# Idle products on a constant, one small product in wider tiles, and a rounding step split by block

## The chip, the cores and the metric

The kernel runs on one core of a Trainium2 chip. The metric is the device time of one execution in microseconds, lower is better. "Span" is the stretch from the first to the last instruction in a profiled execution.

## The reference

Attention with a polynomial sketch (4 batches, 4 heads, 1088 rows, head size 32), then a feed-forward block with an ELU:

```
phi(x) = outer(S1 x, S2 x)                     # 8 x 8 = 64 features
kv = sum_s phi(k_s) v_s^T ;  z = sum_s phi(k_s)
x  = (phi(q) kv) / (phi(q) . z + 1e-6)         # heads side by side: 4352 x 128
h  = x @ w_in                                  # 128 x 2048
out = ELU(h) @ w_out                           # 4352 x 128
```

S1, S2, w_in and w_out arrive as 64-bit floats; the kernel rounds them to 32-bit floats itself, by integer operations on the two words of each number.

## The kernel before

**Tiles and stages.** Rows are worked in groups `g` of 512 (the last of 256). The feed-forward block's 2048 hidden columns are 8 blocks `cp` of 256. For each (g, cp) `mm1` makes `h` in two PSUM banks, `elu` makes `gg` from it (two activations on ScalarE, one VectorE operation), and `mm2`, `mm2_blocks` or `mm2_seven` adds the output product. `steps` lists the pairs (g, cp); the products of a step are written out two steps after its `mm1`.

**Order.** The schedule is manual: each engine runs its instructions in the order in which the program writes them. Ahead of the loop over `steps` stands a prologue written out by hand: features of k and q of the first batch, their sums, the first two groups' queries and the rounding of the first weight blocks. Inside the loop the tables `extra` (filled by `at`, `mid`, `late`) say at which step the other batches' work is put in.

**Tiles of the array.** A product in `quarters` is cut into column tiles of `width[0]` columns (32 at first, 64 from step 30 on); so are `mm2_blocks` and `mm2_seven`. The feature products of the prologue (`KF`, `q1_first`, `q1z_first`, `q1_second`) use tiles of 64 columns, the queries inside the loop tiles of 32 or 64 rows and columns. A 32-bit product is two instructions (two passes) on TensorE for each column tile.

**Idle products.** `keep_warm(n, cols)` issues products of ones in the full 128 x 128 array, whose result in `idle` nobody reads. They stand at the very start (ahead of `sps`, the first product that counts), after `Z(0)`, after the sums of k and v, and ahead of `mm1_first`. Their operand `some` is a 128 x 256 tile that VectorE fills first of all.

**Prologue around the change.** `sps` and `SXps` need `Sx` (rounded S1 and S2). `Sab` comes from `sps`; `KF(0)` makes the features of k in `abp` from `Sab` and the transposed `kT`; `Z_first` sums them into `zps` and copies the sums to `zl`. `Z(0)` multiplies `zl` by `SXh` with `quarters`; `Z_out` writes the masked result into `SW`, from which `q1z_first` makes `zqp`, the denominators' part for the first group's queries. `q2_den` multiplies (`pw`), sums and inverts it (`den`), `q2_out` makes the query features `qp`; `q4_early` transposes them (`qtp`, `qpT`), `q5_early` makes `xps` and `xg`, the input of `mm1`.

**Rounding.** `order` numbers pieces of the weights: 0 and 1 are the w_in halves of blocks 0 and 1, 2 the w_out half of block 0, 3 that of block 1, and so on. `RA`, `RB` make the power of two (VectorE, ScalarE), `RS`, `RM`, `RD` the mantissa, and `RE` multiplies both into `W`. `RC_2` does the last four for pieces 0 and 1 together, in VectorE operations of 512 columns; `RC(i)` does them for one piece.

Of the kernel before, what the change touches and what calls it, by code (L numbers as in the profile page):

```python
# [12 lines left out]
F32 = mybir.dt.float32  # L13
# [9 lines left out]
def _ap(ap: bass.AP, free):  # L23
    return dataclasses.replace(ap, ap=[list(ap.ap[0])] + [list(x) for x in free])
# [3 lines left out]
def kernel(  # L28
# [21 lines left out]
    nc = tc.nc  # L50
    B, H, S, D = q.shape
    R = S1.shape[0]
    P = 128
# [10 lines left out]
    const = ctx.enter_context(tc.tile_pool(name="const", bufs=1))  # L64
# [20 lines left out]
            src = v[b].rearrange("h (y t) d -> y h t d", t=NT)[:, :, t0:t1, :]  # L85
            eng.dma_start(vt[b][r, :VN].rearrange("p (h t d) -> p h t d", h=H, t=KT)[:, :, :t1 - t0, :], src)

    some = const.tile([P, 256], F32, name="some")
    nc.vector.memset(some[:], 1.0)
    idr = const.tile([P, 2 * R, R], F32, name="idr")  # L90
    nc.vector.memset(idr[:], 0.0)
    Sx = const.tile([P, H, D], F32, name="Sx")
# [87 lines left out]
    def round_w(f, i, *a):  # L180
        if wide:
            cp, w_in, w_out = order[i]
            c = slice(0 if w_in else 2 * P, 4 * P if w_out else 2 * P)
            f(raw_w[cp][:, c], W[:, cp, c], *a)

    def RA(i):
        round_w(round_a, i)
# [4 lines left out]

    def RC_2():
        if wide:
            for f in (round_s, round_m, round_d, round_e):
                f(raw_2[:, :, :2 * P], W[:, :2, :2 * P])

    def RS(i):
# [8 lines left out]
    def RE(i):  # L207
        round_w(round_e, i)
# [41 lines left out]
    idle = psum.tile([P, 512], F32, name="idle", tag="o0", bufs=1)  # L250
# [2 lines left out]

    width = [32]

    def quarters(dst, lhs, rhs, **kw):
        for c in range(0, P, width[0]):
            nc.tensor.matmul(dst[c:c + width[0]], lhs[:, c:c + width[0]], rhs, skip_group_check=True,  # L258
                             tile_position=(0, c), **kw)

    def keep_warm(n, cols=256):
        for i in range(n):
            nc.tensor.matmul(idle[:, :cols], some[:, :P], some[:, :cols], skip_group_check=True)  # L263


    nc.gpsimd.tensor_copy(idr[:R], _ap(ident[:R, :R], [[0, 2 * R], [1, R]]))
# [14 lines left out]
    SXh = const.tile([P, FD], F32, name="SXh")  # L281
# [12 lines left out]
    SWq = const.tile([FD, B, 2, 4, R], F32, name="SWq")  # L294
    SWs = const.tile([FD, B - 1, 4, R], F32, name="SWs")
    keep_warm(3)
    keep_warm(1, 128)
    sps = psum.tile([P, 512], F32, name="sps", tag="aux")
    nc.tensor.matmul(sps[:, :2 * R], Sx[:].rearrange("p h d -> p (h d)"), ident[:, :2 * R])
    make_SXh()  # L300
# [102 lines left out]
    def KO_first(t0, t1):  # L403
        half, o = divmod(t0, 5)
        n = t1 - t0
        a_ = kf_ps[half][:, 64 * o:64 * (o + n)].rearrange("p (m x r) -> p m x r", x=2, r=R)[:, :, 1, :]
        b_ = feats[0][:, 0, t0:t1].rearrange("p t h r -> p (t h) r")
        nc.vector.tensor_mul(feats[0, half][:, o:o + n].rearrange("p t h i j -> p (t h) i j"),
                             _ap(a_, list(a_.ap[1:]) + [[0, R]]), _ap(b_, [[R, n * H], [0, R], [1, R]]))
# [30 lines left out]

    def Z(b, ps, zl):

        quarters(ps[:, 96:128], SXh[:], zl[:])

    def Z_out(b, ps):
        z = wzs[b] = SW[:, :, 2, :] if b == 0 else work.tile([FD, H, R], F32, name="wz", tag="wz")[:]
# [22 lines left out]
    def Z_first():  # L469
        ps = psum.tile([P, 512], F32, name="zps", tag="h", bufs=4)  # L470
        for i in range(KT):
            z_tile(0, ps, i)
        return ps, ZC(0, ps)
# [46 lines left out]
    def q1z_first():  # L520
        p = psum.tile([P, 512], F32, name="zqp", tag="h", bufs=4)
        for i in range(4):
            for u in range(2):
                b, t = half_tile(0, 2 * i + u)
                nc.tensor.matmul(p[64 * u:64 * u + 64, i * 32:i * 32 + 32].rearrange("p (h r) -> p h r", h=H),
                                 qT[b][:, t, :], SW[:, :, 2, :], skip_group_check=True, tile_position=(0, 64 * u))
        return p[:, :128].rearrange("p (t h r) -> p h t r", t=4, h=H)
# [58 lines left out]
            nc.vector.transpose(abw[g][:, m * r:m * r + m, :].rearrange("p m y -> p (m y)"),  # L586
                                ps[r][:, o:o + 32 * m])

    def q2(g, parts=1):
        q2_den(g)  # L590
        q2_out(g, parts)

    def q2_den(g, zq=None):
        m = H * (un[g] if g > 1 else qn[g])
        x = abw[g][:, :m, :]
        pw = pws[g % 2]
        if zq is None:
            nc.vector.tensor_mul(pw[:, :m, :R], x[:, :, R:2 * R], x[:, :, 2 * R:3 * R])
        else:
            nc.vector.tensor_mul(pw[:, :m, :R].rearrange("p (h t) r -> p h t r", h=H),  # L600
                                 x[:, :, R:2 * R].rearrange("p (h t) r -> p h t r", h=H), zq)
        den = work.tile([P, 8 * H], F32, name="den", tag="den")
        nc.vector.tensor_reduce(den[:, :m], pw[:, :m], axis=AX, op=ADD)
        nc.vector.reciprocal(den[:, :m], den[:, :m])
        an = work.tile([P, 8 * H, R], F32, name="an", tag="an")
        nc.vector.tensor_mul(an[:, :m], x[:, :, R:2 * R], _ap(den[:, :m], [[1, m], [0, R]]))
        ans[g] = an

    def q2_out(g, parts=1, between=None):
        m = H * qn[g]  # L610
        x, an = abw.pop(g), ans.pop(g)
        qp[g] = work.tile([P, 4 * H, R, R], F32, name="qp", tag="qp", bufs=2)
        for i in range(parts):
            if i and between:
                between()
            h = slice(i * m // parts, (i + 1) * m // parts)
            a_ = an[:, h]
            b_ = x[:, h, :R]
            nc.vector.tensor_mul(qp[g][:, h], _ap(a_, list(a_.ap[1:]) + [[0, R]]),
                                 _ap(b_, [b_.ap[1], [0, R], b_.ap[2]]))  # L620
# [13 lines left out]
    def q5_early(g):  # L634
        xp = [psum.tile([P, 512], F32, name="xps", tag="aux") for _ in range(2)]
        for h in range(H):
            for w in range(2):
                nc.tensor.matmul(xp[w][D * h:D * h + D, :256], kvS[64 * w:64 * w + 64, h, :],  # L638
                                 qpT[g][64 * w:64 * w + 64, h].rearrange("p m s -> p (m s)"),
                                 skip_group_check=True, tile_position=(64 * w, D * h))  # L640
        xg[g] = work.tile([P, 512], F32, name="xg", tag="xg", bufs=3)
        to = xg[g][:].rearrange("p (m w s) -> p w m s", w=2, s=P)
        for w in range(2):
            nc.scalar.copy(to[:, w], xp[w][:, :256].rearrange("p (m s) -> p m s", s=P))
# [210 lines left out]
    def elu_a(g, cp, c, parts=(0, 1)):  # L855

        n = qn[g] * P
        if c == 0 and 0 in parts:
            es[g, cp] = work.tile([P, 2, 512], F32, name="e", tag="e", bufs=2)
        e = es[g, cp][:, c, :n]  # L860
        if 0 in parts:
            nc.scalar.activation(e, hs[g, cp][c][:, :n], RELU, scale=-1.0)  # L862
        if 1 in parts:
            nc.scalar.activation(e, e, EXP, scale=-1.0)  # L864

    def elu_d(g, cp, c):
        n = qn[g] * P
        if c == 0:
            gs[g, cp] = work.tile([P, 2, 512], F32, name="gg", tag="gg", bufs=3)
        nc.vector.scalar_tensor_tensor(gs[g, cp][:, c, :n], es[g, cp][:, c, :n], -1.0, hs[g, cp][c][:, :n],  # L870
                                       op0=ADD, op1=MAX)

    def elu(g, cp, c):
        elu_a(g, cp, c)
        elu_d(g, cp, c)
# [75 lines left out]
    zps, zl = Z_first()  # L951
# [4 lines left out]
    Z(0, zps, zl)  # L956
    Z_out(0, zps)
    KO_first(7, KT)
    keep_warm(1, 96)
    zq = q1z_first()  # L960
    q2_den(0, zq)
    RA(0)
# [6 lines left out]
    q4_early(0)  # L969
    transp(qT, "q", 0, 8, NT)  # L970
    RC_2()
    q5_early(0)
    q1_second()
    keep_warm(1, 192)
    mm1_first()
    RA(2)
    RB(2)
    elu_a(0, 0, 0)
    elu_a(0, 0, 1, (0,))
    q2(1, 2)  # L980
    mm1(0, 1, (0,))
    q4_early(1)
    elu_d(0, 0, 0)
# [116 lines left out]
    N = len(steps)  # L1100
    for n in range(2, N):
        g, cp = steps[n]
        if n == 30:
            width[0] = 64
        mm1(g, cp)
        for f, *a in extra.get(n, ()):
            f(*a)
        elu(g, cp, 0)
        if seven(g, cp):
            sums7(g, cp, 0)  # L1110
        for f, *a in extra.get((n, 0), ()):
            f(*a)
        before = steps[n - 2]
        ends = n > 3 and seven(*before) and before[1] == NP - 1
        if ends:
            elu_a(g, cp, 1, (0,))
            mm2_seven(*before, False, True)
            fin_seven_copy(before[0])
            elu_a(g, cp, 1, (1,))
            fin_seven_a(before[0])  # L1120
            if before[0] == 1:
                fin_seven_b(1)
            elu_d(g, cp, 1)
        else:
            elu(g, cp, 1)
        if seven(g, cp):
            sums7(g, cp, 1)
        if ends and before[0] > 1:
            fin_seven_b(before[0])
        for f, *a in extra.get((n, 1), ()):  # L1130
            f(*a)
        g, cp = before
        if seven(g, cp):
            if cp < NP - 1:
                mm2_seven(g, cp, cp == (NP - 2 if g == 1 else 0), False)
        elif g == 1:
            mm2_blocks(cp)
        elif n > 2:
            mm2(g, cp, cp == 0, cp == NP - 1)
            if cp == NP - 1:  # L1140
                fin1(g)

    g = NQ - 2
# [53 lines left out]
```

## Time and profile before

| What | Value |
|---|---|
| Time, median of 3 runs | 266.83 us (266.22 to 266.89) |
| Profiled execution: its own time, its span | 266.17 us, 264.4 us |
| Busy in the span: TensorE, its weight loads | 258.8 us, 160.6 us |
| Busy in the span: VectorE, ScalarE, GpSimd | 188.5, 184.5, 167.3 us |
| Chain that ended last, TensorE's share | 97% |
| First idle product, `sps`, `mm1_first` begin | 1.19, 4.34, 16.27 us |

In rows of the profile's timeline the first number is the start and the second the duration in microseconds, then the engine (PE is TensorE, PEld its weight load, DVE VectorE, ACT ScalarE, POOL GpSimd), the line, the operation, output and input by their names in the program, for products the rows and columns of the tile in the array, and the shape. In brackets stands how long the engine had been idle, and what released it. In rows of the chain, the duration is followed by the engine, the tile, the line and the number of instructions.

### The profile page before, as it was taken

The page shows a single profiled execution, that of the slowest core. Times are in us where ns is not written, and L with a number is a line of the kernel's source. Part 1 is how long each engine was busy: PE and PEld are TensorE (multiplying, and loading weights), DVE is VectorE, ACT ScalarE, POOL GpSimd, SP SyncE. Part 2 cuts the span into 40 slices and gives each one's busy share as a digit, 9 for nine tenths or more (in the row PEclk, how much of TensorE's full clock was granted, in tenths as well). Part 3 has the DMA queues.
Part 4 walks back from the last instruction along what each step waited for, and adds up shares of the span by engine and source line. Part 5 has one row for each costly group of instructions (what it writes and reads, how often), then busy time and mean ns, then how long its engine had stood idle before and what let it go on. Part 6 is the DMA issues. An engine that isn't in the chain of part 4 may idle for free.

```text
span 264.4 us, 9711 instructions
## 1 busy us (share of the span) xinstructions
PE 258.8 (98%) x4115; PEld 160.6 (61%) x4115; DVE 188.5 (71%) x349; ACT 184.5 (70%) x356; POOL 167.3 (63%) x247
## 2 busy tenths in 40 slices
PE   8899999999999999999999999999999999999994
PEld 7652334354346666667666666665766666667994
DVE  6899999997969997996567675644446445673651
ACT  2469978677567556785587777776777777777792
POOL 4400008203279996798858799898688888998310
PEclk9999999999999999999999999999999999999999
DMA  6997089011011110001100110011001100110021
GB/s 176 333 347 212 2 252 249 6 40 49 2 22 22 29 22 2 2 4 22 26 2 0 24 22 0 2 15 29 3 2 20 24 1 2 18 17 10 2 34 28
DMA packets 26442, 13.73 MB, mean 52 GB/s; under 512 B 19328, under 2 KB 24576, under 8 KB 26400
## 3 DMA queue, kind: packets, MB, share of 16 engines
q1 hardware_dynamic: 25968, 12.76, 18.9%
q8 instruction: 32, 0.52, 0.8%
q10 hardware_dynamic: 368, 0.30, 0.3%
q14 instruction: 10, 0.08, 0.1%
q0 software_dynamic: 64, 0.07, 0.1%
HBM read 10.88 MB, written 2.23 MB: 50 GB/s over the span
## 4 chain that ended last, share of the span: by engine, by line
PE 97%; DVE 1%; ACT 0%; issue 0%; DVEq 0%
PE h L258 44%; PE pb L787 16%; PE pa L787 13%; PE o L258 5%; PE pb L763 4%; PE ol L258 3%; PE idle L263 2%; PE kv L425 1%; PE h L681 1%; PE qps L681 1%; PE kfps L357 1%; PE abp L338 1%; PE qps L573 1%; PE qtp L631 1%; PE kv L258 1%; PE xps L638 0%
## 5 line engine op out<-in xcount | busy, mean ns | idle before, releaser
L258 PE MATMUL h<-xg,W 128*32 128x512 f32 (+3 forms) x896 | 130.7, 539 | 0.0
L870 DVE SCALAR_TENSOR_TENSOR gg<-e,h 128x512 f32<-128x512 f32 x128 | 85.5, 680 | 54.3 <-ACT e L864 50.8
L862 ACT ACTIVATE e<-h 128x512 f32<-128x512 f32 x128 | 75.5, 590 | 46.4 <-PE h L258 42.7
L864 ACT ACTIVATE e<-e 128x512 f32<-128x512 f32 x128 | 80.9, 632 | 3.8
L258 PEld LDWEIGHTS h<-xg,W 128*32 128x32 f32 (+1 forms) x896 | 42.2, 122 | 43.2 <-issue 35.8
L749 POOL TENSOR_TENSOR tt<-gg 128x256 f32<-128x256 f32 x50 | 37.0, 740 | 15.4 <-DVE gg L870 15.1
L746 POOL TENSOR_TENSOR tt<-gg 128x256 f32<-128x256 f32 x50 | 36.7, 734 | 7.8 <-DVE gg L870 7.3
L750 POOL TENSOR_TENSOR tt<-tt,gg 128x256 f32<-128x256 f32 x50 | 37.5, 750 | 3.9
L751 POOL TENSOR_TENSOR tt<-gg,tt 128x256 f32<-128x256 f32 x50 | 37.1, 743 | 3.9
L787 PEld LDWEIGHTS pa<-gg,W 128*64 128x64 f32 (+1 forms) x496 | 23.8, 125 | 23.5 <-issue 22.9
L787 PE MATMUL pa<-gg,W 128*64 128x128 f32 (+1 forms) x496 | 30.5, 274 | 0.0
L787 PE MATMUL pb<-tt,SS 128*64 128x128 f32 (+1 forms) x480 | 29.5, 273 | 0.0
L787 PEld LDWEIGHTS pb<-tt,SS 128*64 128x64 f32 (+1 forms) x480 | 22.6, 126 | 0.0
L787 PE MATMUL pa<-tt,SS 128*32 128x128 f32 (+1 forms) x288 | 21.1, 273 | 0.0
L135 POOL TENSOR_TENSOR raw<-raw,tiny 128x512 f32<-128x512 f32 x1 | 1.0, 1041 | 29.9 <-DVE raw L130 29.9
L787 PE MATMUL pb<-gg,SS 128*64 128x128 f32 (+1 forms) x256 | 19.8, 273 | 0.0
L787 PE MATMUL pb<-tt,W 128*64 128x128 f32 (+1 forms) x256 | 19.8, 273 | 0.0
L258 PE MATMUL o<-gg,W 128*32 128x512 f32 x128 | 15.3, 594 | 0.0
L787 PEld LDWEIGHTS pa<-tt,SS 128*32 128x32 f32 (+1 forms) x288 | 13.5, 123 | 0.3 <-POOL tt L750 0.3
L787 PEld LDWEIGHTS pb<-gg,SS 128*64 128x64 f32 (+1 forms) x256 | 12.6, 125 | 0.0
L787 PEld LDWEIGHTS pb<-tt,W 128*64 128x64 f32 (+1 forms) x256 | 12.6, 125 | 0.0
L763 PE MATMUL pb<-gg,W 128*32 128x256 f32 x192 | 11.5, 380 | 0.0
(164 smaller groups left out, 279.6 us busy)
## 6 DMA issues: line engine op xcount, KB each, us to landing
raw<-in_moe_w_in_dram SPq DMA_DIRECT2D x8, 256.0 KB, 6.8
raw<-in_moe_w_out_dram SPq DMA_DIRECT2D x8, 256.0 KB, 6.8
hd_k<-in_k_dram SPq DMA_DIRECT2D x3, 544.0 KB, 6.8
hd_q<-in_q_dram SPq DMA_DIRECT2D x3, 544.0 KB, 8.0
out_dram<-ob SPq DMA_DIRECT2D x88, 16.0 KB, 1.5
v<-in_v_dram SPq DMA_DIRECT2D x4, 288.0 KB, 6.3
v<-in_v_dram SPq DMA_DIRECT2D x4, 256.0 KB, 8.1
hd_k<-in_k_dram SPq DMA_DIRECT2D x1, 288.0 KB, 3.4
```

What stands on the lines that cost most here:

```text
L258: nc.tensor.matmul(dst[c:c + width[0]], lhs[:, c:c + width[0]], rhs, skip_group_check=True, tile_position=(0, c), **kw)
L263: nc.tensor.matmul(idle[:, :cols], some[:, :P], some[:, :cols], skip_group_check=True)
L681: nc.tensor.matmul(ps[w][s * r:s * r + s, 64 * k:64 * (k + m)], lhs, qpT[g, i][rows, o + 2 * k:o + 2 * (k + m), f, :], start=(f == 0 and j ...
L746: nc.gpsimd.tensor_tensor(t[:, 0], b12, b11, op=SUB)
L749: nc.gpsimd.tensor_tensor(t[:, 2], b22, b12, op=SUB)
L750: nc.gpsimd.tensor_tensor(t[:, 1], t[:, 2], b11, op=ADD)
L751: nc.gpsimd.tensor_tensor(t[:, 3], b21, t[:, 1], op=SUB)
L763: nc.tensor.matmul(acc[1][0][r:r + width[0], 256 * hi:256 * hi + 256], lhs[:, w:w + width[0]], gg[:, c, 256 * u:256 * u + 256], start=(cp ...
L787: nc.tensor.matmul(bank[r:r + width[0], P * col:P * col + P], lhs[:, w:w + width[0]], rhs[:, u], start=(first and i in ((0,) if g == 1 els ...
L862: nc.scalar.activation(e, hs[g, cp][c][:, :n], RELU, scale=-1.0)
L864: nc.scalar.activation(e, e, EXP, scale=-1.0)
L870: nc.vector.scalar_tensor_tensor(gs[g, cp][:, c, :n], es[g, cp][:, c, :n], -1.0, hs[g, cp][c][:, :n], op0=ADD, op1=MAX)
```

## The change

- `some` and its fill are gone. `keep_warm` reads a constant of ones instead: one column that the program's preamble fills, read again for each of the columns. It takes a `tile` width: with less than 128, each idle product is cut into column tiles.
- The idle product ahead of `sps` has 224 columns instead of 128. That after `Z(0)` is cut into tiles of 64 columns, that ahead of `mm1_first` into tiles of `width[0]` = 32.
- `Z(0)` uses tiles of 64 columns; `Z` of the other batches keeps `width[0]`.
- `RC_2` no longer does the last step; `RE(0)` and `RE(1)` follow it, each for its own block.
- `q2(1, 2)` stands where `RA(2)` stood, and `RA(2)` runs inside it, between the first multiplication of `q2_den` and its sum. `RB(2)` and the first `elu_a` calls come after.
- At step 30 `width[0]` becomes 64 after `mm1` and the step's extra work, instead of before.

```diff
-    some = const.tile([P, 256], F32, name="some")
-    nc.vector.memset(some[:], 1.0)
...
-            for f in (round_s, round_m, round_d, round_e):
+            for f in (round_s, round_m, round_d):
                 f(raw_2[:, :, :2 * P], W[:, :2, :2 * P])
...
-    def quarters(dst, lhs, rhs, **kw):
-        for c in range(0, P, width[0]):
-            nc.tensor.matmul(dst[c:c + width[0]], lhs[:, c:c + width[0]], rhs, skip_group_check=True,
+    def quarters(dst, lhs, rhs, tile=None, **kw):
+        tile = tile or width[0]
+        for c in range(0, P, tile):
+            nc.tensor.matmul(dst[c:c + tile], lhs[:, c:c + tile], rhs, skip_group_check=True,
                              tile_position=(0, c), **kw)
...
-    def keep_warm(n, cols=256):
+    def keep_warm(n, cols=256, tile=P):
+        ones = nc.const_aps.tensor(1.0, [P, 256], F32)
         for i in range(n):
-            nc.tensor.matmul(idle[:, :cols], some[:, :P], some[:, :cols], skip_group_check=True)
+            for c in range(0, P, tile):
+                nc.tensor.matmul(idle[c:c + tile, :cols], ones[:, :tile], ones[:, :cols], skip_group_check=True,
+                                 tile_position=(0, c))
...
     keep_warm(3)
-    keep_warm(1, 128)
+    keep_warm(1, 224)
...
-        quarters(ps[:, 96:128], SXh[:], zl[:])
+        quarters(ps[:, 96:128], SXh[:], zl[:], None if b else 64)
...
-    def q2(g, parts=1):
-        q2_den(g)
+    def q2(g, parts=1, between=None):
+        q2_den(g, None, between)
         q2_out(g, parts)
 
-    def q2_den(g, zq=None):
+    def q2_den(g, zq=None, between=None):
...
+        if between:
+            between()
         den = work.tile([P, 8 * H], F32, name="den", tag="den")
...
-    keep_warm(1, 96)
+    keep_warm(1, 96, 64)
...
     RC_2()
+    RE(0)
+    RE(1)
     q5_early(0)
     q1_second()
-    keep_warm(1, 192)
+    keep_warm(1, 192, width[0])
     mm1_first()
-    RA(2)
+    q2(1, 2, lambda: RA(2))
     RB(2)
     elu_a(0, 0, 0)
     elu_a(0, 0, 1, (0,))
-    q2(1, 2)
...
-        if n == 30:
-            width[0] = 64
         mm1(g, cp)
         for f, *a in extra.get(n, ()):
             f(*a)
+        if n == 30:
+            width[0] = 64
```

## The prediction

> **What bounds the kernel.** I read the page's busy shares and its chain first: from early on TensorE is the limit, so only what moves TensorE's own sequence counts, and a microsecond gained early is kept if nothing behind it is later than TensorE.
>
> ```profile
> PE 258.8 (98%) x4115; PEld 160.6 (61%) x4115; DVE 188.5 (71%) x349; ACT 184.5 (70%) x356; POOL 167.3 (63%) x247
> PE 97%; DVE 1%; ACT 0%; issue 0%; DVEq 0%
> ```
>
> The stage windows agree: from 23.35 to 127.90 us PE is busy 104.54 of 104.55, from 132.20 to 260.90 all of 128.70. What is left lies before 23.35, and in the price of a product. Next, the timeline of the start (POOL, DVE and PE in turn), and the windows of the tile `abp` (stretch, its length, PE's busy time and instructions in it):
>
> ```profile
> 0.28 0.10 POOL L1182 MEMSET const-float32-1.0<- 128x1 f32 x1
> ...
> 0.87 0.27 DVE L89 MEMSET some<- 128x256 f32 x1 [0.87 <-PEq L1182]
> ...
> 3.71 0.28 DVE L272 SCALAR_TENSOR_TENSOR Sx<-raw_s,S 16x128 f32<-16x128 f32 x1
> ...
> 1.19 3.36 PE L263 MATMUL idle<-some 128*128 128x256 f32 x8 [1.19 <-DVE some L89]
> 4.34 0.45 PE L299 MATMUL sps<-ident,Sx 128*128 128x16 f32 x2
> ```
>
> ```profile
> 5.40:5.90 0.50, 0.50 (x5) 0.50 (x6) 0.00 (x0) 0.00 (x0) 1.00 0.98 322
> 6.10:6.60 0.50, 0.50 (x21) 0.50 (x19) 0.00 (x0) 0.00 (x0) 1.00 1.01 223
> ```
>
> The first idle product waits for the fill of `some`. `sps` waits for idle products, not for `Sx`, which is done at 3.99. In half a microsecond, 5 `abp` products run at 5.4 but 21 at 6.1: near 6.0 PE became about twice as fast (the page's PEclk row is at 9 throughout and doesn't show it). Third, the timeline around `Z(0)` and around the first `mm1`:
>
> ```profile
> 8.56 0.27 PE L258 MATMUL zps<-zl,SXh 128*32 128x32 f32 x8
> ...
> 8.97 0.19 DVE L447 TENSOR_TENSOR SW<-zps,bmask 128x32 f32<-128x32 f32 x1 [0.55 <-PE zps L258]
> ...
> 15.39 0.69 DVE L138 SCALAR_TENSOR_TENSOR W<-raw,W 128x512 f32<-128x512 f32 x1
> ...
> 15.75 0.59 PE L263 MATMUL idle<-some 128*128 128x192 f32 x2
> 15.87 0.48 ACT L538 COPY abw<-abwp 128x384 f32<-128x384 f32 x1
> ...
> 16.27 0.64 PE L258 MATMUL h<-xg,W 128*32 128x256 f32 x8
> ```
>
> `mm1_first` begins at 16.27; W is complete at 15.39 + 0.69 = 16.08, `xg` at 15.74. Last, the chain around step 30, where the products' width changes:
>
> ```profile
> 127.98 1.87 PE h L258 x8
> ...
> 133.92 1.72 PE h L258 x8
> ```
>
> The first 64-wide `h` step takes 0.15 us more than the next one.
>
> **What the Trainium skill says.** "TensorEngine Tiling (Array Packing)", Key Properties: a change of tiling mode drains TensorE. The trace agrees: 0.15 us at step 30. "TensorE: Matmul & The Clock Gate", Part 1: the array starts at half clock, and a free-running window of activity, 3.4 us long, releases it; where the window lies differs from run to run. The trace agrees: idle passes of 256 columns start 0.43 us apart (1.78, 2.21, 2.64), while 256-column passes of `mm1_first` later start 0.216 apart, and the release is seen about 4.8 us after the first product. "Perfetto Trace Analysis", Optimizing Scalar/DVE Operations: a VectorE operation on SBUF costs some 60 ns whatever its size; the trace has 0.69 us for 512 columns and 0.42 for 256 (L138), with the next one starting about 0.06 before an end, so a pair costs 0.78 against 0.69.
>
> **The parts, by the profiled execution** (span 264.40, own time 266.17, so 1.77 around the span).
>
> *Start.* `some` and its 0.27 us fill go. The constant is filled at 0.28 to 0.38, ahead of the barrier after which engines start at 0.74 to 0.87. The first product then starts at about 0.83, 0.36 earlier. But 96 columns more run there: in two passes at the half clock, 2 x 96 x (0.4267/256) = 0.32. So `sps` comes 0.04 earlier (0 to 0.08, by the start taken). `Sab` also follows the transpose of `kT` (DVE 4.58 to 4.90), but `abp` starts only at 5.33, behind `SXps`; **0.04**. DVE's chain to `Sx` gains nothing: it waits for `raw_s` until 2.31, which covers the lost fill. The release of the clock: the first product is 0.36 earlier, so on average the release is too. Half of that, 0.1 to 0.2, would be gained in `abp` where release falls inside it, nothing where it falls elsewhere; in one run it may be unmoved. I take 0 in this execution.
>
> *Z(0).* Before it stand 64-wide products (`abqp`, last pair at 8.41, pairs 0.058 apart in the timeline taken in narrow stretches), after it a 64-wide one. In 32-wide tiles `zps` starts at 8.562. In 64-wide ones it needs no drain: 8.468 and 8.526 for the two passes, end at 8.526 + 0.007 + 0.222 = 8.755 against 8.831. `SW` follows by 0.14 as now and is in turn what `zqp` waits for (9.16 to 9.21). The idle product in 64-wide tiles (four instructions, two passes x 0.08) ends before 8.9 and stays hidden in that wait. **0.08**, and it is carried by DVE (`pw`, `den`, two `qp`), ACT (`qpT`) and PE (`xps`, `abwp`) to 16.27; their DMAs have landed (the weights of blocks 0 and 1 at 9.70 and 10.51, first used at 11.21 and 12.01).
>
> *Rounding by block.* L138 of 512 columns becomes two of 256. Block 0 is done at 15.39 + 0.42 = 15.81 instead of 16.08, `xg` stays at 15.74. Now PE ends last: `abwp`'s last product at 15.575, a change to 32-wide at 15.75 (as now to the full width), then two passes of 192 columns, 0.186 and 0.16: `mm1_first` at 16.10 without a further change of mode, against 16.27. **0.17**; 0.1 if the first pass fills as slowly as now (0.27), 0.27 if all of the earlier W counted. Block 1 is done 0.09 later, used from 18 us on.
>
> *q2(1) ahead, RA(2) within.* DVE does `pw`, then RA(2) (0.29, about 0.21 of the queue), then `den`. `pw` still starts at 16.38 because it waits for ACT's `abw` (15.87 + 0.48); the longer rounding ends at 16.17. The gap of 0.10 between `pw` and `den` takes most of RA(2); `den`, `an` and both `qp` come 0.03 later. Queued behind RA(2): RB(2) on ACT, from 16.33 to about 16.93, ending 17.44; behind it `elu_a`, whose products are due at 17.62. Covered by 0.18. `qp`'s second half ends at 19.05, its transposes would want it at 19.49 - 0.17 = 19.32. Then `gg` 18.97 instead of 19.13, RC(2) with it, W's out half at 21.26; `o` wants it at 21.61 - 0.17 = 21.44. Cost **0**; if one of these covers is thin, up to the 0.17.
>
> *Width at step 30.* `h` of step 30 stays 32-wide, at 1.72 as in the steps before; the queries after it change mode in both kernels, the step's `mm2` goes to 64-wide in both. One change fewer: **0.15** (0.1 to 0.2, not seen: a 32-wide step followed by 32 x 32 query tiles at this place).
>
> Sum: 0.04 + 0.08 + 0.17 + 0.15 = **0.44**: 266.17 becomes 265.73. That execution was among the fast ones: 266.22, 266.83, 266.89 were the timed runs. The release of the clock, which moves by itself, is my reading of that spread (one more microsecond of half clock inside `abp` costs about 0.5). So I set the sum against the mean of the four, 266.53: **266.1**, which is 0.27% under the median of 266.83.
>
> **Rivals.**
> *The clock is released a good deal earlier.* For: about 40% of a 3.4 us window was busy before; 0.36 us more may fill it enough. Limit: `abp` also waits for `kT`, transposed until 6.36, so at most about 0.3 on top in this execution, and more against a late run: 265.5.
> *The early gains are given back.* PE's head start of 0.25 meets a later wait: `o` for RC(2)'s W or for `gg` (their weight loads wait for DVE now, 0.41 and 0.52), or the dependency of `mm1_first` covers the whole of W, so that RE(1) at 16.17 binds. Against the latter: `abp` starts at 5.33 with transposes of the same tile still to come. Then step 30, the start and some of Z remain, 0.2: 266.4.
> *Slower: the constant is read slowly.* It is one column read again and again by the weight load and the stream; no product of this trace does so. The idle products stand straight before `sps`, with no slack: `Sx` is ready 0.3 earlier. They last 3.3 us; the whole gain is gone at 13% longer, and from 37% (1.24 us) the kernel is over 0.3% slower. At half the rate, part of it then at full clock, 2 to 3.3 us: 268.5. Against: nothing in the trace ties PE's rate to addresses; idle passes run at the clock's pace alone.
> That the change doesn't start earlier at all (some other wait at PE's start) is within the forecast: 96 more columns would then cost 0.32, leaving 0.1.
>
> **Numbers.** A measurement tells about 0.3%, 0.80 us: faster is below 266.03, slower above 267.63. Forecast 0.55, own range 265.6 to 266.6, 0.25 of it below 266.03; clock earlier 0.16, all faster; given back 0.19, all within; slow constant 0.10. So faster 0.41, within 0.49, slower 0.10. The range 265.4 to 266.9 leaves out the slow constant and some 0.07 at the fast end.
>
> **What would show it.** First idle product near 0.83 and its passes 0.43 apart: the start; `sps` past 4.4: slow constant. `zps` with 4 products near 8.4, `SW` 0.08 earlier. Two L138 of 0.42, `mm1_first` 0.2 to 0.3 earlier, the same lead at `o` (21.3) and at 127. Step 30's `h` at 1.72, a lead of 0.4 after it. If the lead at 127 is under 0.15, the second rival holds; if `abp` runs fast from its start, the first.

## The result, and the profile after

Over 8 runs each, the changed kernel takes 265.89 us (265.60 to 266.19), the kernel before 266.44 (266.16 to 266.89). The ratio is 0.9978, 95% interval 0.9969 to 0.9987: 0.22% faster, 0.55 us, clear of no change and short of 0.3%. The forecast was 266.1, range 265.4 to 266.9, and a sum of 0.44 us. That range also holds the unchanged kernel's 266.44, so the total alone doesn't test the forecast; its parts do.

The profiled execution of the changed kernel took 266.09 us, though, only 0.08 less than that of before, so its page looks the same:

```profile
PE 258.8 (98%) x4127; PEld 160.8 (61%) x4127; DVE 188.2 (71%) x349; ACT 184.3 (70%) x356; POOL 167.1 (63%) x247
PE 96%; POOL 1%; DVE 1%; ACT 0%; issue 0%
```

Where the gain is has to be read stretch by stretch. The starts below are from PE's timeline, taken in narrow stretches and from first product to first product; "again" is a later execution of the same changed kernel.

| Stretch (us) | before | after | again |
|---|---|---|---|
| span's start to `abp` | 5.333 | 5.260 | 5.057 |
| `abp` to `zps` | 2.002 | 2.320 | 2.050 |
| `zps` to the last `abqp` | 1.075 | 1.075 | 1.078 |
| last `abqp` to `zqp` | 0.802 | 0.676 | 0.675 |
| `zqp` to `abwp` | 5.728 | 5.732 | 5.729 |
| `abwp` to `mm1_first` | 1.333 | 1.164 | 1.164 |
| `mm1_first` to `o` | 5.334 | 5.307 | 5.308 |
| `o` to the last product ahead of step 30 | 106.097 | 106.126 | 106.130 |
| that product to step 30's queries | 2.070 | 1.919 | 1.919 |
| queries to the last product's end | 131.131 | 131.138 | 131.137 |

Three stretches got shorter by the same amount in both executions: 0.126, 0.196 (two rows: 0.169 + 0.027) and 0.151. `o` to step 30 is 0.03 longer in both; it differs between traces anyway: 106.09 to 106.14 in nine of the fourteen traces, 106.18 to 106.34 in the other five, where the cause wasn't followed. `abp` differs most from execution to execution. The start, in PE's timeline after:

```profile
0.78 3.65 PE L265 MATMUL idle<-const-float32-1.0 128*128 128x256 f32 x8 [0.78 <-PEq L1188]
4.22 0.50 PE L302 MATMUL sps<-ident,Sx 128*128 128x16 f32 x2
```

The first idle product starts 0.41 earlier, `sps` 0.12, `abp` 0.07. The windows of `abp` (stretch, length, PE's busy time and instructions) show what this execution lost:

```profile
5.40:5.90 0.50, 0.50 (x6) 0.50 (x7) 0.00 (x0) 0.00 (x0) 1.00 0.90 278
6.10:6.60 0.50, 0.50 (x12) 0.50 (x12) 0.00 (x0) 0.00 (x0) 1.00 1.13 264
6.80:7.30 0.50, 0.50 (x20) 0.50 (x16) 0.00 (x0) 0.20 (x1) 1.00 1.16 283
```

Before, 21 instructions fell into the stretch from 6.1; here 12 do, and the quick pace comes later. A 64-column `abp` product lasts 0.314 us at the slow pace and 0.222 at the quick one; the step between them is what is called the release of the clock here. It falls at about 5.95 us before and 6.5 here, and `abp` to `zps` is 0.32 longer.

`Z(0)` and the first `mm1`, timeline after:

```profile
8.71 0.26 PE L257 MATMUL zps<-zl,SXh 128*64 128x32 f32 x4
...
9.08 0.19 DVE L450 TENSOR_TENSOR SW<-zps,bmask 128x32 f32<-128x32 f32 x1 [0.42 <-PE zps L257]
...
15.52 0.76 DVE L136 SCALAR_TENSOR_TENSOR W<-raw,W 128x256 f32<-128x256 f32 x2
15.87 0.16 PEld L265 LDWEIGHTS idle<-const-float32-1.0 128*32 128x32 f32 x8
15.87 0.53 PE L265 MATMUL idle<-const-float32-1.0 128*32 128x192 f32 x8
...
16.23 0.83 PE L257 MATMUL h<-xg,W 128*32 128x256 f32 x12
```

`mm1_first` comes 0.36 after the idle product's start where it came 0.52 after, and 0.71 after the rounding's last step starts (before: 0.88). In the chain around step 30 the longer step is gone:

```profile
127.93 1.72 PE h L257 x16
...
133.73 1.72 PE h L257 x8
```

### The profile page after: what moved, and what is told of

Same layout as the page of the kernel before. It is cut to its first block, busy times and chain, and to the rows that moved or that the text cites. A ratio compares the mean times of both kernels' runs of the same rounds, so it can differ in the third digit from the quotient of the medians.

```text
span 264.3 us, 9735 instructions
## 1 busy us (share of the span) xinstructions
PE 258.8 (98%) x4127; PEld 160.8 (61%) x4127; DVE 188.2 (71%) x349; ACT 184.3 (70%) x356; POOL 167.1 (63%) x247
## 4 chain that ended last, share of the span: by engine, by line
PE 96%; POOL 1%; DVE 1%; ACT 0%; issue 0%
PE h L257 44%; PE pb L792 16%; PE pa L792 13%; PE o L257 5%; PE pb L768 4%; PE ol L257 3%; PE idle L265 2%; PE kv L428 1%; PE h L686 1%; PE qps L686 1%; POOL kp L324 1%; PE kfps L360 1%; PE qps L576 1%; PE abp L341 1%; PE qtp L636 1%; PE kv L257 1%
```

## The experiments

All start from the changed kernel. The first four are one profiled execution each (265.52 to 266.18 us), to be read by their stretches and not by their times.

**Two parts undone, 120 us apart** (`u_z32_width`)

```diff
-        quarters(ps[:, 96:128], SXh[:], zl[:], None if b else 64)
+        quarters(ps[:, 96:128], SXh[:], zl[:])
...
+        if n == 30:
+            width[0] = 64
         mm1(g, cp)
         for f, *a in extra.get(n, ()):
             f(*a)
-        if n == 30:
-            width[0] = 64
```

> Two parts undone at places 120 us apart: Z(0) in 32-wide tiles again, and width 64 from ahead of step 30's mm1. Theory (each part is worth a change of tiling mode at its own place): from the last abqp product to the first zqp product 0.80 us as in the kernel before, against 0.68 in the changed kernel; step 30's h takes 1.87 us again instead of 1.72. Rival (what came 0.13 earlier at zqp came from the idle product's tiles or from the other edits): the first stretch stays at 0.68 to 0.72. The time of one look tells nothing here: both parts together are about 0.25 us.

From the last `abqp` product to `zqp` 0.804 us. Its timeline and its chain:

```profile
8.74 0.27 PE L257 MATMUL zps<-zl,SXh 128*32 128x32 f32 x8
8.94 0.39 PE L265 MATMUL idle<-const-float32-1.0 128*64 128x96 f32 x4
9.39 0.31 PE L528 MATMUL zqp<-SW,qT 128*64 128x32 f32 x4
```

```profile
127.98 1.87 PE h L257 x8
```

Each part is worth what stands at its own place: 0.128 for Z(0)'s tiles (the idle product behind it stayed in 64-wide tiles and made no difference), 0.151 for step 30 (2.070 against 1.919). Of the 0.128, 0.10 lies ahead of the first `zps` product: it starts 0.152 after the last `abqp` product in 32-wide tiles, 0.052 in 64-wide ones.

**The rounding joined again** (`u_joined`)

```diff
-            for f in (round_s, round_m, round_d):
+            for f in (round_s, round_m, round_d, round_e):
...
     RC_2()
-    RE(0)
-    RE(1)
```

> The last rounding step of blocks 0 and 1 joined again in one VectorE operation of 512 columns; the idle product ahead of mm1_first stays in 32-wide tiles. From the first abwp product to the first mm1 product: 1.33 us in the kernel before, 1.16 in the changed one. Theory (TensorE's change of mode was the later of the two, W the earlier by little): W is complete at 0.69 instead of 0.42 after the operation's start, some 0.27 later, and mm1_first starts about 1.22 after abwp: a third of the gain goes. Rival 1 (the split is the gain): 1.33. Rival 2 (mm1_first waits for all of W in both kernels): 1.16, unchanged.

**The idle product in the full array again** (`u_idle_full`)

```diff
-    keep_warm(1, 192, width[0])
+    keep_warm(1, 192)
```

> The idle product ahead of mm1_first in the full array again, on the constant; the rounding stays split by block. Theory (mode changes and the fill after them bind): from the first abwp product to the first mm1 product 1.33 us as in the kernel before, although W's block 0 is ready 0.27 earlier, and mm1_first itself 0.025 longer again (2.72 to the next transposes instead of 2.70). Rival (the split is the gain): 1.16 to 1.20.

`abwp` to `mm1_first`: 1.290 joined, 1.336 with the full array, against 1.333 before and 1.164 with both parts. `mm1_first` itself, up to the next transposes, took 2.724 and 2.723 in the two, as before, against 2.697. The 0.027 lies nearly all in its first pass, after a change of mode or a wait for W: the eighth product starts 0.260 after the first in these three, 0.235 in the changed kernel ("fill" below). The timelines, joined first:

```profile
15.03 0.69 DVE L136 SCALAR_TENSOR_TENSOR W<-raw,W 128x512 f32<-128x512 f32 x1
...
15.39 0.53 PE L265 MATMUL idle<-const-float32-1.0 128*32 128x192 f32 x8
...
15.87 0.64 PE L257 MATMUL h<-xg,W 128*32 128x256 f32 x8
```

```profile
15.05 0.76 DVE L136 SCALAR_TENSOR_TENSOR W<-raw,W 128x256 f32<-128x256 f32 x2
...
15.41 0.59 PE L265 MATMUL idle<-const-float32-1.0 128*128 128x192 f32 x2
...
15.94 0.64 PE L257 MATMUL h<-xg,W 128*32 128x256 f32 x8
```

Joined, W ends at 15.72 and `mm1_first` follows 0.15 later, weight load and fill first; PE's passes of the idle product were through at about 15.74 and would have let it start then. In the full array, W's first block is ready at 15.48, but PE gets through its idle product and the change of mode only at 15.94. In the kernel before, two gates stood within 0.05 us of each other: opening W's alone (`u_idle_full`) brought nothing, opening PE's alone (`u_joined`) 0.04, both 0.169, and 0.027 more within `mm1_first`.

**RA(2) ahead of q2(1) again** (`u_ra2_first`)

```diff
-    q2(1, 2, lambda: RA(2))
+    RA(2)
     RB(2)
     elu_a(0, 0, 0)
     elu_a(0, 0, 1, (0,))
+    q2(1, 2)
```

> RA(2) ahead of q2(1, 2) again, with RB(2) and the first elu_a calls written between them, everything else as in the changed kernel. Theory (this part is worth nothing, as forecast): pw starts when abw is there, within 0.03 of the changed kernel, the second qp ends within 0.05, and o starts equally far after the first mm1 product, 5.31 us, within 0.02. Rival (the move is needed to keep the gain): qp or W's out half comes over 0.1 later and o starts 5.4 or more after the first mm1 product.

`abwp` to `mm1_first` 1.163, `mm1_first` to `o` 5.307, as in the changed kernel, and the second `qp` ends 2.92 us after `mm1_first` begins in both. This part is worth nothing.

**The changed kernel once more** (`after_again`)

> The changed kernel unchanged, beside the others. Theory: 0.5 us under the kernel before, with the release of the clock somewhere between 2.9 and 5.7 us after the first product at 0.78, and zps between 7.05 and 7.6 accordingly; all later stretches as in its first trace within 0.03. Rival (the later release of its first trace, 5.7 us after the first product, is what the constant operand does): release again later than 6.2.

265.84 us (265.55 to 266.17, 10 runs) against 266.38 before, ratio 0.998 (0.997 to 0.9989). In its profile, of an execution of 265.60, the clock was released at 3.6, during the idle products, and PE's timeline shows the quick pace from `sps` on:

```profile
4.33 0.36 PE L302 MATMUL sps<-ident,Sx 128*128 128x16 f32 x2 [0.21 <-DVE Sx L275]
4.54 0.47 PE L288 MATMUL SXps<-Sx,idr 128*128 128x128 f32 x2
5.06 0.33 PE L341 MATMUL abp<-Sab,kT 128*64 128x64 f32 x2
```

So the constant does not bring the late release: one kernel had it 5.7 us and 2.8 us after its first product. Here `zps` came at 7.11, the end 0.47 earlier than in the first trace.

**Fewer idle columns ahead of sps** (`x_start128`, `x_start176`)

```diff
-    keep_warm(1, 224)
+    keep_warm(1, 128)
```

> The changed kernel with 128 instead of 224 columns in the last idle product ahead of sps. Theory (the idle products delay sps while the clock is at half; Sx is ready at 3.99): at half clock sps at about 4.06 instead of 4.22 and abp at 5.10 instead of 5.26; where the clock is released before SXps, abp starts at 5.0 as it does with 224. zps no earlier than 7.0, because kT's transposes end at 6.36. In time at most 0.1 us less than the changed kernel, within the noise: 265.8. Rival (the longer idle product is what gets the clock released in time): release later on average and 0.2 us or more slower than the changed kernel.

267.13 us (266.60 to 267.52, 6 runs), ratio to before 1.0025 (1.0013 to 1.0037): the theory missed by 1.3 us, and the time moved as the rival had it. In the profiled execution, of 267.17, PE had a pause ahead of `sps`, and `abp` kept the slow pace to its end. PE's timeline and the windows of `abp`:

```profile
3.05 1.06 PE L265 MATMUL idle<-const-float32-1.0 128*128 128x256 f32 x3
4.33 0.58 PE L302 MATMUL sps<-ident,Sx 128*128 128x16 f32 x2 [0.22 <-DVE Sx L275]
```

```profile
5.50:6.00 0.50, 0.50 (x5) 0.50 (x6) 0.00 (x0) 0.00 (x0) 1.00 1.08 311
6.20:6.70 0.50, 0.50 (x12) 0.50 (x11) 0.00 (x0) 0.00 (x0) 1.00 1.07 222
7.20:7.70 0.50, 0.50 (x13) 0.50 (x10) 0.00 (x0) 0.18 (x1) 1.00 1.11 221
```

`sps` itself was no earlier: `Sx` was done at 4.18 here (3.99 in the first trace of the changed kernel, but 4.18 in `after_again` too, where its input landed as late), and its weight load follows only then. The release falls between 8.45 and 8.8, some 7.8 after the first product. With 176 columns:

> The changed kernel with 176 columns in the last idle product ahead of sps, halfway between the 224 of the changed kernel and the 128 that took 1.3 us more. Theory (TensorE's pause between the idle products' end and sps, and the two thin sps products after it, spoil a window of activity, so that the clock is released a window later): idle ends at about 4.06, the pause is 0.27 or less instead of 0.43, so most executions get the early release and some don't: times in two clumps near 265.8 and 267.1, a median between. Rival (the count of columns decides): about 0.65 over the changed kernel, 266.5, without clumps.

Twelve of 14 runs took 265.53 to 266.03, two took 267.07 and 267.25; median 265.74. Two clumps, as the theory has it; the median itself is no different from the changed kernel's. The one trace is of a run of 265.87, so what made the two long runs isn't shown.

**No idle products ahead of sps** (`x_no_start_idle`)

```diff
-    keep_warm(3)
-    keep_warm(1, 224)
```

> The changed kernel without any idle product ahead of sps. Theory (the clock is released 2.9 to 5.7 us after the first product, as in the five traces so far, whatever that product is): first product sps at about 4.06, release between 7.0 and 9.8, all of abp at half clock, zps at about 8.3 to 8.9 instead of 7.05 to 7.6; 1.0 to 2.0 us slower than the changed kernel, 267.0 to 268.0. Rival (the release comes at a fixed time of the execution, not after the first product): release before 6.8 and no more than 0.4 slower.

266.91 us (13 runs), ratio 1.0022 (1.0014 to 1.003), 1.07 over the changed kernel: the lower end of the theory. All of `abp` ran at the slow pace (2.813 to `zps`, which came at 8.07, a little ahead of the 8.3 expected), release near 8.8. The four idle products are worth 1.07 us; with 128 columns in the last of them they were worth nothing.

**More idle columns ahead of sps** (`x_start320`)

```diff
-    keep_warm(3)
-    keep_warm(1, 224)
+    keep_warm(4)
+    keep_warm(1, 64)
```

> The changed kernel with 96 columns more ahead of sps (64 columns and four products of 256). Theory (224 columns already leave no pause that counts): release as in the changed kernel, 2.9 to 5.7 us after the first product; sps at 4.54 instead of 4.22 where the clock is still at half, abp 0.3 later there; 0.1 to 0.3 us slower than the changed kernel, 266.0 to 266.15. Rival (more columns go on bringing the release forward): as fast as the changed kernel or faster, 265.6 to 265.85.

266.07 us (265.57 to 266.41, 22 runs). The median is some 0.2 over the changed kernel's, within the theory's range, but the runs of the two overlap too far to tell this from no difference. No gain shows, against the rival. In its trace `sps` came at 4.65 and the release near 6.4.

**Sx late** (`x_sx_late`)

```diff
+        late_sx = const.tile([P, 384], F32, name="late_sx")
+        nc.vector.memset(late_sx[:], 0.0)
         nc.vector.scalar_tensor_tensor(Sx[:2 * R], ...
```

> The changed kernel, all 224 columns kept, with a VectorE fill of 384 columns (some 0.4 us) put just ahead of the operation that writes Sx: sps comes about 0.5 later, after a pause of TensorE of about 0.5 between the idle products' end at 4.22 and sps. Theory (the pause spoils the window, not the count of columns): most executions get the release only after 7.6, abp at half clock to its end, 1.1 to 1.9 us slower than the changed kernel, 267.0 to 267.8; a few that were released before the pause near 266. Rival (the count of columns decides, the pause doesn't matter): the delay alone, at most 0.5: 266.0 to 266.35, as with 96 columns more, where abp came 0.3 to 0.5 later.

265.94 us; 11 of 14 runs lie between 265.45 and 266.27, three at 267.32 to 267.33. Neither expectation holds. The fill delayed `Sx` by 0.24, not 0.4, and `sps` came at 4.37: a pause of 0.15, not 0.5. A clump of long runs with all 224 columns would speak for the pause, but no trace of one of these runs was taken, and the next experiment shows another way to such a time. So this stays open.

**No idle product ahead of mm1_first** (`x_no_idle_mm1`, `x_no_idle_look`)

```diff
-    keep_warm(1, 192, width[0])
```

> The changed kernel without the idle product ahead of mm1_first. Theory (after the change this idle product, not W, is what mm1_first waits for): abwp to mm1 1.00 us instead of 1.164, mm1_first itself 0.025 longer for its fill; then gg, which already follows qp without a gap on VectorE, stays where it is, and o starts only about 0.1 earlier than in the changed kernel: 0.1 us off the time, 265.8. Rival 1 (all 0.17 kept): mm1 to o 5.33 or less. Rival 2 (the idle product keeps the clock up): passes of mm1_first at 0.43 instead of 0.216, time 1 us or more longer.

265.81 us (22 runs), ratio 0.9979 (0.9972 to 0.9986): the same as the changed kernel, so the second rival falls. Its profiled execution took 267.19, and its chain shows another way to such a time:

```profile
1.93 5.61 DMA hd_q<-in_q_dram
...
7.56 0.72 DVE qT L281
```

The first block of q landed at 7.54, in the first profile of the kernel before at 6.50. The clock was not late here: `abp` ran at the quick pace from about 5.7. So the long runs with 176 columns and with `Sx` late may have come from either cause. A second profiled execution of this kernel:

> A second look at the changed kernel without the idle product ahead of mm1_first, because the profiled execution of the first was 1.4 us over the median of that kernel, with VectorE late throughout. Theory: abwp to mm1 1.00 us instead of 1.164, then mm1 to o 5.38 or more instead of 5.31, because gg and RC(2) on VectorE don't move; o starts 0.05 to 0.1 earlier after abwp than in the changed kernel. Rival (W by block is later than the idle product anyhow): abwp to mm1 1.14 to 1.19, nothing moved, as its time of 265.81 would fit.

```profile
15.26 0.76 DVE L136 SCALAR_TENSOR_TENSOR W<-raw,W 128x256 f32<-128x256 f32 x2
...
15.83 1.07 PE L257 MATMUL h<-xg,W 128*32 128x256 f32 x16
```

`abwp` to `mm1_first` 1.026: `mm1_first` now follows W's first block (15.26 + 0.42 = 15.68) by 0.15, as it followed the whole of W in `u_joined`. `mm1_first` to `o` took 5.357, short of the 5.38 expected; `o` comes 0.09 earlier after `abwp` than in the changed kernel. Of that 0.065 was lost again within the next 9 us. So the theory held in the main, 0.02 was left, and no version better than the changed kernel came of it.

## Why the prediction was right

- **Width at step 30**: 0.15 forecast, 0.151 measured.
- **Z(0)**: 0.08 forecast, 0.126 measured. The place was right, the term too small. `zps` followed `abqp` at 0.052 (0.058 forecast), its second pass came 0.031 after the first, not the 0.058 taken over from the 64-column `abqp`, and `SW` started 0.117 after `zps` ended, not 0.137.
- **Rounding by block**: 0.17 forecast at `mm1_first`, 0.169 measured, and 0.027 more, which the forecast didn't have, because `mm1_first` no longer starts with a fill. The forecast read the order of the gates rightly (PE last, W by little); `u_idle_full` and `u_joined` show that neither edit does it alone.
- **q2(1) ahead, RA(2) within**: 0 forecast, 0 measured.
- **Clock released a good deal earlier** (the first rival): open in part. Its sign, `abp` quick from its start, is missing in the first trace of the changed kernel but stands in `after_again`, `u_joined` and `u_ra2_first`. Its limit held: the earliest `zps`, at 7.05, is 0.28 ahead of the 7.335 before, where 0.3 was named. Whether the release comes earlier on average than before isn't shown, since there is one trace of the kernel before.
- **Given back later** (the second rival): no. In the changed kernel `mm1_first` to `o` got no longer, and what follows kept its length within 0.03, apart from step 30. Only a further 0.14 at `mm1_first` found the next waits. The sign named for this rival, a lead under 0.15 at 127 us, did appear in the first pair of traces (127.66 against 127.70), but from the late clock: that sign didn't tell the two apart.
- **Slow constant**: no. Idle passes of 256 columns start 0.427 apart in both kernels (1.34, 1.77, 2.19 after).
- **Start**: 0.04 forecast, 0.07 measured at `abp` where both ran at the slow pace. The release of the clock stood in the sum as 0. The three fixed parts make 0.126 + 0.196 + 0.151 = 0.473, or 0.44 if the 0.03 at `o` to step 30 is taken off; the medians differ by 0.55 and, in the second set, 0.54. Some 0.1 is left for start and clock together, with an uncertainty of about 0.2 on it. One thing the forecast missed here: it had the 96 added columns only as a cost of 0.32. Without them the kernel is slower than before (267.13 against 266.38), so they decide whether the whole change gains. That the start came out near its forecast owes something to luck.
- **Spread as the clock's**: mostly borne out. In nine traces with 224 or 176 idle columns and without the added fill, the release fell between 2.8 and 5.7 us after the first product, and `zps` came between 7.05 and 7.58. Late landing of a DMA is a second source, and the stretch from `o` to step 30 (up to 0.25 between traces) a third; the prediction named neither.

## What to carry to other kernels

A change of tiling mode on a busy TensorE cost 0.10 to 0.15 us here, so put neighbours in the same tiles and cut fillers to their neighbours' tiles. Idle products that are to bring the quick pace should be tried at several lengths, up to the first product that counts: 96 columns fewer cost 1.3 us here. Where a product waits for two things within 0.05 us of each other, undo or do both before judging either. When two profiled executions differ by less than one kernel's executions do among themselves, compare them stretch by stretch, not by their totals.

## What the runs showed of the hardware beyond that

- The release in traces with idle products up to `sps` came 2.8, 2.9, 3.5, 4.7, 5.2 and 5.7 us after the first product, among others; an early one also lets `abp` start at 5.01 to 5.06 instead of 5.26. Earlier than about 5.5 it no longer helped `zps`: with releases at 3.6, 3.7, 4.25 and 5.45 us of the span, `zps` started at 7.11, 7.09, 7.05 and 7.09, while `kT` was transposed until 6.28 to 6.33.
- With 128 columns ahead of `sps`, one trace has a pause of 0.43 us (the last idle pass, started at 3.69, is through at 3.90 by the pace of the passes, at 4.11 by the profile's modelled end; `sps` starts at 4.33), then the two `sps` products of 16 columns, and a release some 7.8 us after the first product. All six runs were long, 266.60 to 267.52, 1.3 us in the median. That it is the pause, rather than the missing columns, isn't shown: in that trace `Sx` came 0.19 later than in most others, so the other runs may have had a shorter pause, and no trace tells what made the long runs with 176 columns and in `x_sx_late`.
- One column of ones, read again for each column, keeps the pace of a filled tile: passes of 256 columns start 0.427 us apart with either, at the slow pace.
